# Two rings for attention weights in place of one, with the k/v ring 64 bytes lower in SBUF

## The chip, the cores and the metric

The kernel runs on one core of a Trainium2 chip. The metric is device microseconds of one execution, as the median of several runs; a profiled execution gives the trace that all lines below come from. The engines are TensorE (PE, with its weight loads shown as PEld), VectorE (DVE), ScalarE (ACT), GpSimd (POOL) and SyncE (SP), whose queue issues every DMA of this kernel. Each engine runs its own instructions in order and waits on semaphores for the others.

## What is computed

One transformer-like block on x of 2048 tokens by 1024 channels, in float32: a modulated layer norm, an attention with a compressive memory over four segments of 512 tokens (32 heads of 32), a gated residual, then a second modulated layer norm, a token-mixing MLP and a gated residual.

```python
mod = (_silu(c) @ w_mod)                       # six rows: sa, ca, ga, sb, cb, gb
h = _layernorm(x) * (1 + ca) + sa
# attention: q, k, v = h @ wq, h @ wk, h @ wv, 32 heads, 4 segments of 512
for s in range(4):
    p = softmax(qs @ ks.T * scale + mask)
    a_mem = (phi(qs) @ M) / (phi(qs) @ z + 1e-6)
    o = g * a_mem + (1 - g) * (p @ vs)
    M, z = M + phi(ks).T @ vs, z + sum(phi(ks))
x = x + ga * (o @ wo)
h = _layernorm(x) * (1 + cb) + sb
x = x + gb * (W2 gelu(W1 LayerNorm(h)^T + b1) + b2)^T
```

## The kernel before

**Precision.** A matrix that must be exact is kept as two fp32r halves, high and low: `split` (L116 to L123) copies the high half with one engine (L120 when that is ScalarE) and subtracts it with another (L123). A product is then three matmuls: high by high, high by low, low by high.

**Attention.** The heads are taken in 8 groups of four. `its` (L306) lists 32 projects: in pass 0 each group has segments 0 and 1, in pass 1 each group has segments 2 and 3. So the two projects 2g and 2g+1 use one set of weights, and a group comes back in the second pass.

- The normalised input lies in `page` tiles `h` (a ring of 16, 4 KB a partition each), as 8 chunks of 128 channels.
- `project` (L322) has four pieces. Pieces 0 and 1 compute k and v for half of the segment each: `kv_chunk` (L178) runs 48 matmuls at L185, with a 128x128 block of `h` stationary and 256 columns of the k/v weights moving (`nps`). Piece 2 transposes k (`kps`, L356), then `q_chunk` (L189) runs 24 matmuls at L193, with the q weights stationary and 512 columns of `h` moving (`qps`); k and q are split into `sg`, and `stack` (L312) sends parts of `sg` to the tiles `sk` with three DMAs a head. Piece 3 stacks the last head and works on the memory M.
- A step of the loop at L563 handles one head: `scores` (matmuls L446 to L453, exp on ScalarE, a mask and a second half on POOL, L457 and L461), `maxima` (L424, L425) for three steps ahead, `values` (L475) for the step before, and a piece of a project eight steps ahead.

**Weights.** A group has six weight tiles of 4 KB a partition, four for k/v (`v`, two parts of two) and two for q. They come from one ring of eight buffers (pool `paw`, tag `w`, L156). `load_w` (L168) is called four steps before the group's first project. In pass 0 `load_part` (L149) loads 512 KB into a `raw` buffer (a ring of three, shared with the loads of `token_tile`, `mod_late` and `wo_ahead`) and splits it into two tiles, each with a ScalarE copy and a VectorE subtract; `keep_w` (L163) then writes the six tiles to DRAM (`wsp`). In pass 1 the tiles are read back from `wsp` by the DMAs at L160. A tile of the ring may be written again only after the last matmul that reads its predecessor in the buffer.

**Addresses.** A pool is a stretch of SBUF, the same in every partition, and pools are stacked. `pad`, `pad2` (L71, L72) and `offset` are tiles that nothing reads or writes; they only shift what follows. `acst` holds `pad2` and small constants (mask, bd, csb, saca, MZ, bdg), and `paw` follows it.

**Order.** The kernel text gives the order in which instructions are recorded. A scheduler that works with its own model of times then interleaves them on each engine; `issue_after` and priorities bound it. So a changed dependency can move instructions that the diff doesn't touch. DMAs take eight semaphores in turn, and each waits for the eighth before it to be complete.

Of the kernel before, what the change touches and what calls it, by code (L numbers as in the profile page):

```python
# [7 lines left out]
F32 = mybir.dt.float32  # L8
F32R = mybir.dt.float32r
# [9 lines left out]
P = 128  # L19
# [25 lines left out]
def attention_and_mlp(ctx, tc, x, wq, wkv, wo, beta, w1, b1, w2, b2, c, wm_a, wm_b, out):  # L45
# [22 lines left out]
    acst = acst_pool.__enter__()  # L68
    top_pool = tc.tile_pool(name="top", bufs=1, side="right")
    top = top_pool.__enter__()  # L70
    top.tile([P, 8], F32, name="pad")  # L71
    acst.tile([P, 24], F32, name="pad2")  # L72
    psum = ctx.enter_context(tc.tile_pool(name="psum", bufs=1, space=PSUM))

    def bank(tag, bufs, name):
# [40 lines left out]
    def split(dst, src, hi_eng, lo_eng):  # L116

        hi, lo = dst[:, 0], dst[:, 1]
        if hi_eng is A:
            A.copy(hi, src)  # L120
        else:
            hi_eng.tensor_copy(hi, src)
        lo_eng.tensor_tensor(lo, src, hi.bitcast(F32), op=ALU.subtract)  # L123
# [20 lines left out]

    paw = tc.tile_pool(name="paw", bufs=1)
    aw = paw.__enter__()
    raw_w = {}

    def load_part(g, pr, kind, part, res):  # L149


        if pr == 0:
            r = a.tile([P, D], F32, tag="raw", bufs=3, name=f"raw{kind}{g}_{part}")
            SY.dma_start(r, (wkv if kind == "v" else wq)[g, :, 1024 * part:1024 * part + 1024])
        for i in range(2):
            w = aw.tile([P, 2, 512], F32R, tag="w", bufs=8, name=f"w{kind}{pr}_{g}_{part}_{i}")  # L156
            if pr == 0:
                split(w, r[:, 512 * i:512 * i + 512], A, V)
            else:
                SY.dma_start(w.bitcast(F32), wsp[g, 2 * part + i if kind == "v" else 4 + i])  # L160
            res[kind, 2 * part + i] = w
# [6 lines left out]
    def load_w(g, pr):  # L168
        res = W[pr, g] = {}
        for kind, part in (("v", 0), ("v", 1), ("q", 0)):  # L170
            load_part(g, pr, kind, part, res)
        if pr == 0:
            keep_w(g)
# [93 lines left out]
    for ct in range(NK):  # L267
        for part in range(2):
            wm = s1p.tile([P, D], F32, tag="wm", bufs=11, name=f"wm{ct}_{part}")
            last_wm = SY.dma_start(wm, wm_a[part, ct])  # L270
            if part == 0:
                V.scalar_tensor_tensor(wm, wm, 1.0, scb, op0=ALU.mult, op1=ALU.mult, accum_out=saca[:, ct, 0:1])
            else:
                for k in range(NK):
                    T.matmul(scale_ps[:, ct:ct + 1], wm[:, P * k:P * k + P], sc[:, k:k + 1], start=(k == 0),
                             stop=(k == NK - 1), skip_group_check=True)
        if ct < 3:
            load_part(0, 0, *(("v", 0), ("q", 0), ("v", 1))[ct], W[0, 0])
        V.tensor_scalar_add(saca[:, ct, 1:2], scale_ps[:, ct:ct + 1], 1.0)
        h_chunk(s1p, xs[0], 0, ct)  # L280
        if ct:
            first_chunk(ct - 1)
    first_chunk(NK - 1)
    left.__exit__(None, None, None)
    prj = tc.tile_pool(name="prj", bufs=1, reuse_waits="tile")
    pj = prj.__enter__()
    late = tc.tile_pool(name="late", bufs=1, reuse_waits="tile")
    b = late.__enter__()
    skp = [tc.tile_pool(name=f"sk{i}", bufs=1, reuse_waits="tile") for i in range(2)]
# [273 lines left out]
    for n in range(-LEADS, 4 * NI + VL):  # L563
# [19 lines left out]
        if 4 * NI - 5 <= m < 4 * NI + 3:  # L583
            i = m - 4 * NI + 5
# [5 lines left out]
        if n >= ML0 and (n - ML0) % MLS == 0 and (n - ML0) // MLS < 32:  # L590
            mod_late((n - ML0) // MLS)
    right.__exit__(None, None, None)
    for q in skp + [late, prj, paw]:
        q.__exit__(None, None, None)


# [6 lines left out]
    w = cw_pool.__enter__()  # L603
# [344 lines left out]
```

## Time and profile before

| | us |
|---|---|
| median of 3 runs | 2335.71 (2332.09 to 2339.83) |
| the profiled execution | 2329.09 |
| its span, first to last instruction | 2327.4 |
| TensorE busy in it | 2244.8 (96%) |
| VectorE, ScalarE, POOL busy | 1693.3, 1107.6, 721.8 |

Its mean granted TensorE clock is 0.983. TensorE's largest groups, mean time of one matmul from start to end (they are pipelined, so less than that lies between two starts):

| line | what | count | busy us | mean ns |
|---|---|---|---|---|
| L745 | the MLP's matmuls, 512 columns, three groups | 4704 | 535.6 + 431.7 + 164.5 | 389 |
| L185 | k and v, 256 columns | 3072 | 447.6 | 287 |
| L193 | q, 512 columns | 768 | 200.1 | 408 |
| L653 | output projection, 512 columns | 768 | 184.0 | 398 |
| L475 | probabilities by values, 97 or 65 columns | 2560 | 156.9 | 205 |

In the page's chain of what ended last, TensorE has 82% of the span, DMAs 6%, VectorE 6%. Attention runs to about 1020 us, the output projection to about 1200 us, and the MLP to the end.

A few times of single projects, from the trace: the k/v matmuls of project 3 end at 126.2 us, its q matmuls run from 145.7 to 152.0, and the q matmuls of project 4, the first of the next group, start at 173.3. In pass 1, the k/v matmuls of project 27 end at 898.5, its q matmuls at 907.4, and project 28's q matmuls start at 929.4.

### The profile page before, as it was taken

What the parts mean: (1) busy time and instruction counts of PE and PEld (TensorE: products, weight loads), DVE (VectorE), ACT (ScalarE), POOL (GpSimd) and SP (SyncE); (2) the same over time, 40 slices, a digit from 0 to 9 for tenths busy, and PEclk for the clock granted to TensorE, in tenths of its full rate; (3) what the DMA queues carried; (4) which work ended last, traced back from release to release, by engine and by line L of the source; (5) the groups of instructions that cost most, each with busy time, mean ns of one, the idle gap of its engine ahead of it and who ended that gap; (6) DMA issues with size and microseconds to landing.
All of it is one profiled execution on the core that took longest, in us unless ns stands there. A gap on an engine that the chain in (4) does not pass through costs nothing.

```text
span 2327.4 us, 38419 instructions
## 1 busy us (share of the span) xinstructions
PE 2244.8 (96%) x13866; PEld 1931.2 (83%) x13866; DVE 1693.3 (73%) x3806; ACT 1107.6 (48%) x2010; POOL 721.8 (31%) x827
## 2 busy tenths in 40 slices
PE   8999999999899999998989999999999999999999
PEld 7888888888789999986877888888888788888887
DVE  5666666785776566657889666598889787868687
ACT  5476766655566666655324333353335242424232
POOL 3165555675676555555000000023332000000000
PEclk9999999999999999999999999999999999999999
DMA  6747565788774444374354765465557542423233
GB/s 245 247 122 217 179 185 150 231 295 271 219 218 121 122 119 120 105 238 139 128 195 166 285 227 211 147 251 212 213 213 270 186 136 78 140 69 128 67 116 147
DMA packets 172593, 414.67 MB, mean 178 GB/s; under 512 B 17236, under 2 KB 71540, under 8 KB 163444
## 3 DMA queue, kind: packets, MB, share of 16 engines
q1 hardware_dynamic: 172404, 412.22, 53.3%
q8 instruction: 110, 1.80, 0.3%
q14 instruction: 79, 0.65, 0.1%
HBM read 236.23 MB, written 125.06 MB: 155 GB/s over the span
## 4 chain that ended last, share of the span: by engine, by line
PE 82%; DMA 6%; DVE 6%; ACT 2%; POOL 2%; issue 2%; SPq 1%; DVEq 0%; POOLq 0%; ACTq 0%
PE mx L745 44%; PE nps L185 12%; PE qps L193 7%; PE po L653 6%; PE pv L475 3%; PE sx L424 1%; PE a L446 1%; PE sz L424 1%; DMA rawx<-in_x_dram 1%; DMA rawm<-in_wm_b_dram 1%; PE a L449 1%; DMA wor<-in_wo_dram 1%; PE rd L396 1%; PE a L453 1%; PE up L406 1%
## 5 line engine op out<-in xcount | busy, mean ns | idle before, releaser
L745 PE MATMUL mx<-bU,sp 128*128 128x512 f32 x2352 | 535.6, 389 | 2.6 <-DVE sp L123 1.3
L745 PEld LDWEIGHTS mx<-bU,sp 128*128 128x128 f32 x2352 | 440.9, 188 | 96.8 <-DVE sp L123 2.1
L185 PE MATMUL nps<-wv,h 128*128 128x256 f32 x3072 | 447.6, 287 | 1.3 <-POOL h L123 1.1
L745 PE MATMUL mx<-bA,sp 128*128 128x512 f32 x1764 | 431.7, 389 | 3.4 <-DVE sp L123 1.8
L120 ACT CAST sp<-wr 128x384 fp32r<-128x384 f32 (+2 forms) x408 | 217.3, 545 | 445.5 <-PE mx L745 377.5
L461 POOL TENSOR_TENSOR ph<-p,ph 128x640 f16<-128x640 f32 x256 | 374.5, 1484 | 148.8 <-ACT ph L459 143.4
L185 PEld LDWEIGHTS nps<-wv,h 128*128 128x128 f32 x3072 | 409.8, 192 | 6.3 <-POOL h L123 1.3
L745 PEld LDWEIGHTS mx<-bA,sp 128*128 128x128 f32 x1764 | 330.7, 188 | 73.6 <-DVE sp L123 2.6
L123 DVE TENSOR_TENSOR sp<-wr,sp 128x384 fp32r<-128x384 f32 (+2 forms) x408 | 261.0, 651 | 33.7 <-ACT sp L120 33.2
L752 DVE TENSOR_TENSOR ac<-mx,ac 128x512 f32<-128x512 f32 x280 | 190.4, 689 | 91.0 <-PE mx L745 90.3
L193 PE MATMUL qps<-h,wq 128*128 128x512 f32 x768 | 200.1, 408 | 1.4 <-DVE r L349 1.3
L459 ACT CAST ph<-p 128x1280 f16<-128x1280 f32 x128 | 160.8, 1257 | 69.9 <-POOL p L457 69.3
L653 PE MATMUL po<-wo,ots 128*128 128x512 f32 x768 | 184.0, 398 | 8.1 <-DVE x L656 5.9
L653 PEld LDWEIGHTS po<-wo,ots 128*128 128x128 f32 x768 | 146.5, 192 | 40.1 <-issue 6.7
L193 PEld LDWEIGHTS qps<-h,wq 128*128 128x128 f32 x768 | 147.0, 197 | 31.8 <-issue 1.7
L457 POOL TENSOR_SCALAR_AFFINE_SELECT p<-p 128x256 f32<-128x256 f32 x256 | 126.1, 501 | 138.5 <-ACT p L454 88.4
L475 PE MATMUL pv<-vp,ph 128*128 128x97 bf16 (+1 forms) x2560 | 156.9, 205 | 10.8 <-POOL ph L461 4.5
L425 DVE CUSTOM_DVE_ANT_0 sx<-sx,mask 128x128 f32<-128x128 f32 (+1 forms) x256 | 110.5, 432 | 75.0 <-PE sx L424 73.8
L745 PE MATMUL mx<-bB,sp 128*128 128x512 f32 x588 | 164.5, 389 | 0.0
L475 PEld LDWEIGHTS <-ph 128*128 128x128 f16 x2560 | 121.0, 100 | 40.4 <-issue 17.1
L752 DVE TENSOR_TENSOR cc<-mx,cc 128x512 f32<-128x512 f32 x140 | 94.6, 685 | 53.4 <-PE mx L745 48.4
L745 PEld LDWEIGHTS mx<-bB,sp 128*128 128x128 f32 x588 | 110.3, 188 | 23.3 <-ACT bB L120 0.4
(173 smaller groups left out, 3184.6 us busy)
## 6 DMA issues: line engine op xcount, KB each, us to landing
sk<-sg SPq DMA_DIRECT2D x384, 128.0 KB
wr<-in_w_dram SPq DMA_DIRECT2D x28, 1024.0 KB
wr<-in_w_dram SPq DMA_DIRECT2D x32, 768.0 KB
bstu<-ucd SPq DMA_DIRECT2D x28, 768.0 KB
wsp<-wv SPq DMA_DIRECT2D x32, 512.0 KB
rawm<-in_wm_b_dram SPq DMA_DIRECT2D x32, 512.0 KB
wv<-wsp SPq DMA_DIRECT2D x32, 512.0 KB
pcd<-cc SPq DMA_DIRECT2D x14, 1024.0 KB
```

What stands on the lines that cost most here:

```text
L120: A.copy(hi, src)
L123: lo_eng.tensor_tensor(lo, src, hi.bitcast(F32), op=ALU.subtract)
L185: T.matmul(ps[:, aa], h[:, j, 128 * tt:128 * tt + 128], wt[:, i, o:o + 256], start=(n == 0), stop=(n >= 6 * NK - 2), skip_group_check=True)
L193: T.matmul(ps, wt[:, i, o:o + 128], h[:, j], start=(k + n == 0), stop=(3 * k + n == 3 * NK - 1))
L425: V.tensor_tensor_reduce(o, o, mask[:, 384 - 128 * i:], 1.0, -3.0e38, op0=ALU.add, op1=ALU.max, accum_out=mx[:, h % 2, i:i + 1])
L457: G.affine_select(w, w, pattern=[[0, 2], [1, 128]], compare_op=ALU.is_ge, fill=0.0, base=0, channel_multiplier=-1)
L459: A.copy(ph[:, 0], p32)
L461: G.tensor_tensor(ph[:, 1, c], p32[:, c], ph[:, 0, c], op=ALU.subtract)
L475: T.matmul(pv[:, i, 0:w], ph[:, part, o:o + 128], d["vp"][:, j, h, 0:w], start=(n == 0), stop=(n == 19), skip_group_check=True)
L653: T.matmul(ps, os_[:, i, P * ct:P * ct + P], wop[ct, nh][:, j], start=(n == 0), stop=(n == 3 * NK - 1))
L745: T.matmul(ps, ops[q][:, i, P * k:P * k + P], b[:, j], start=(m == 0 and first), stop=(m == 3 * nk - 1), skip_group_check=True)
L752: V.tensor_tensor(d, ps, d, op=ALU.add)
```

## The change

The one ring of eight becomes two pools: `paw`, now with six buffers for the k/v tiles, and after it `paq`, with an unused tile of 64 bytes and two buffers for the q tiles. `pad2` shrinks from 96 to 32 bytes, so what lies between it and the rings, and the k/v ring, starts 64 bytes lower; the unused tile puts the q ring and all behind it at the addresses they had.

```diff
-    acst.tile([P, 24], F32, name="pad2")
+    acst.tile([P, 8], F32, name="pad2")
...
     paw = tc.tile_pool(name="paw", bufs=1)
     aw = paw.__enter__()
+    paq = tc.tile_pool(name="paq", bufs=1)
+    awq = paq.__enter__()
+    awq.tile([P, 16], F32, name="pad3")
...
         for i in range(2):
-            w = aw.tile([P, 2, 512], F32R, tag="w", bufs=8, name=f"w{kind}{pr}_{g}_{part}_{i}")
+            w = (aw if kind == "v" else awq).tile([P, 2, 512], F32R, tag="w", bufs=6 if kind == "v" else 2,
+                                                  name=f"w{kind}{pr}_{g}_{part}_{i}")
...
-    for q in skp + [late, prj, paw]:
+    for q in skp + [late, prj, paq, paw]:
         q.__exit__(None, None, None)
```

## The prediction

> **What bounds the kernel now.** I read the table of stages first: busy time of each engine in four stretches, granted clock, DMA share, GB/s.
>
> ```profile
> core 0: us, PE busy (x) PEld busy (x) DVE busy (x) ACT busy (x) POOL busy (x), PEclk, DMA share, GB/s
> 100.00:700.00 600.00, 560.18 (x4687) 506.24 (x4686) 411.20 (x1213) 388.48 (x715) 367.70 (x405) 0.95 0.68 209
> 700.00:1010.00 310.00, 310.00 (x2759) 285.83 (x2757) 188.18 (x641) 192.65 (x339) 181.29 (x247) 1.00 0.45 127
> 1200.00:2327.00 1127.00, 1114.13 (x4899) 918.05 (x4897) 886.91 (x1461) 398.57 (x730) 96.88 (x60) 1.00 0.48 173
> ```
>
> TensorE (PE) ends last everywhere. From 700 to 1010 us (pass 1 of attention) it is never idle and its clock is 1.00: there only the speed of a matmul counts. From 100 to 700 (pass 0 and the start of pass 1) it is idle for 600 - 560.2 = 39.8 us and the clock averages 0.95: there a late producer shows. After 1200 us come the MLP's L745 matmuls, which touch no k, v or q weight.
>
> Next, the timeline of TensorE in pass 1, for the rate of one matmul. Columns: start, length, instruction, count.
>
> ```profile
> 814.76 4.04 PE L193 MATMUL qps<-h,wq 128*128 128x512 f32 x17
> 818.64 0.22 PE L452 MATMUL a<-sk 98*128 98x128 f32 x1
> ...
> 821.36 1.47 PE L185 MATMUL nps<-wv,h 128*128 128x256 f32 x11
> 822.67 0.34 PE L449 MATMUL a<-sk 98*128 98x384 f32 x1
> ```
>
> From the first start to the start of what follows: 17 q matmuls take 3.88 us, 228 ns each; 11 kv matmuls take 1.31 us, 119 ns each. 256 columns more cost 109 ns, so about 10 ns of each is not columns.
>
> Last, who makes and uses the q weights (name, median of one in ns between least and most, first and last start), and SyncE's (SP's) issues near one group change of pass 1.
>
> ```profile
> L193 PE MATMUL qps<-h,wq x768: 387/389/776, 28.0 to 1021.7; 128*128 128x512 f32 x192
> L120 ACT CAST wq<-rawq x16: 602/618/632, 18.7 to 462.9; 128x512 fp32r<-128x512 f32 x16
> L123 DVE TENSOR_TENSOR wq<-rawq,wq x16: 679/717/1506, 19.4 to 467.1; 128x512 fp32r<-128x512 f32 x16
> L160 SPq DMA_DIRECT2D wq<-wsp x16: 320/382/418, 536.5 to 956.9; - x16
> ```
>
> ```profile
> 898.76 0.86 SPq L160 DMA_DIRECT2D wq<-wsp  x2
> 899.99 0.32 SPq L493 DMA_DIRECT2D oT<-ot  x1
> 904.00 0.32 SPq L160 DMA_DIRECT2D wv<-wsp  x1
> 906.30 1.88 SPq L437 DMA_DIRECT2D sk<-nt  x3
> ```
>
> The two q loads went out at 898.76 and 899.2, as soon as the last k/v matmuls of project 27 had read the slots. The v load at 904.00 waited for a q tile of that project to be read: the one ring shows itself.
>
> **The change part by part.** *Work.* Each engine has the same instructions, none added or removed but waits; the two pads are allocated and never written. Cost 0.
>
> *Addresses.* All weights, the h pages and later tiles lie 224 bytes past a multiple of 256 now. The k/v ring moves to 160, the q ring stays at 224, and so does all behind. The small constants between pad2 and the rings (mask, bd, MZ, bdg) move by 64 bytes too. So the 3072 kv matmuls (L185) read moving weights and stationary h 64 bytes apart modulo 256; q matmuls as before. No fp32r matmul in this trace has its operands off the same residue, so this is bounded from both sides. The gain ends where the 10 ns above the columns are gone: 3072 x 10 = 31 us. For the loss I let that overhead double: 31 us. The nearest row is pv (L475), whose moving operand starts at many offsets against its stationary one: matching the trace's records to the program's addresses, the step from one 97-column matmul to the next has its median at 43 to 46 ns, differs with the address modulo 16 and not with the distance modulo 256. 64 is a multiple of 16. I take 0.
>
> The Trainium skill (TensorE: Matmul & The Clock Gate, "Step-by-step: what each phase is for") says that weight loads and moving data have two independent read ports, so that a load takes no bandwidth from a running matmul. By it this term is 0 for any distance. No run here shows fp32r operands 64 bytes apart.
>
> *The rings.* One ring of 8 held 6 tiles of a group and 2 to spare, the spare being the next group's first two v tiles. Now v has 4 and 2 to spare, q has 2 and none. So the next q tiles wait for the last q matmuls of the group's second project, not for its k/v matmuls; and the next-but-one group's first v tiles no longer wait for those q matmuls.
>
> In pass 1 the two loads of the row above wait for 904.0 and 907.4 (the last readers in project 27) instead: 5.2 and 8.2 us later. The next q matmuls start at 929.4. 1 MB at that stage's 127 GB/s is 8.3 us: there by 916, 13 us early. The new program places the first v loads ahead of them. Behind the waiting loads are two sk<-nt rows that come at 906.3 anyway; the second pair would be held 0 to 1 us, and their reader is several head steps on. Cost 0; without the 13 us it would be the lateness itself.
>
> In pass 0 a q tile is a ScalarE copy (0.62 us) and a VectorE subtract (0.72) from a raw buffer. There are six changes where the wait binds (groups 2 to 7). At before's times, the copies would be 1 to 26 us late, and stand in the new order inside the q matmuls of the group's second project, the second copy just ahead of the sg copy that reads those matmuls. The next q matmuls come some 21 us later (152.0 to 173.3 us between projects 3 and 4), so the tile itself is in time. What is queued behind pays: the ScalarE waits, held against before's end times of its neighbours, are 1.0, 1.1, 0.5, 3.4, 0 and 3.1 us; but the 3.4 is a place where ScalarE sat idle for 4.05 us on the same matmuls anyway. The other five average 1.1. So at most 6 x (0.62 + 0.72 + 1.1) = 15 us, if each us reached TensorE; at least 0, if the sg chain's slack hides it (the scores that need it come several head steps later). TensorE was idle only 40 of 600 us here, so most lands beside its work: I take a quarter, +4. If that cover is gone, the exp of the next scores (L447 to L454) is late, then POOL's L461, then pv.
>
> *The order.* The scheduler interleaves differently from about 129 us: some 6,800 of 16,170 TensorE program entries stand elsewhere, most by a few places, and almost none after 1200 us. It can give or take from the 40 us of idle time and the 30 us that a clock of 0.95 costs in that stretch (600 x 0.05). Bounds: a seventh of 70 either way, 10 us, as most entries keep their neighbours. I take 0.
>
> *Sum.* 0 + 0 + 0 + 4 + 0 = +4 us on the profiled execution's 2329.1 (span 2327.4): 2333. That execution is 6.6 us under the median of the runs, 2335.7; against that the time is 2340.
>
> **The rivals.** *B, the q split becomes the wait in pass 0.* All 15 us reach TensorE: 2335.7 + 15 = 2351. For it: ScalarE and VectorE are in-order, busy 388 and 411 of 600 us; a raw buffer held longer delays the rawm loads, for which VectorE waited 30.3 us in this stretch. Against it: the new order was made with that wait in it. It decides once a held-up copy outlasts the scores already queued for TensorE. The Trainium skill (same page, "What's actually happening") adds that an idle window of about 3.4 us halves the clock; the trace agrees so far that the clock is 1.00 where TensorE is never idle, 0.95 where it is idle 7%.
>
> *C, 64 bytes speed the kv matmuls.* Price up to 31 us; with two thirds of the 10 ns gone, -20: 2316. For it: fp32r matmuls of both lengths carry the same overhead, all with operands on one residue, and pv carries less (43 ns for 97 columns, which are 41 at the same rate). Against it: pv's indifference to distance.
>
> *D, the same 64 bytes slow them.* Half of 31, with the +4: 2356; the same facts, the other sign.
>
> *E, the new order or the earlier v tiles fill idle time.* -10: 2326. For it: v loads free of the q matmuls, and DMA waits in the chain (5.4 us on rawv at 194, 7.1 on rawm at 228). Against: raw buffers, not weight slots, held those.
>
> **How the numbers follow.** Forecast A 0.40 (2340), B 0.24, C 0.17, D 0.07, E 0.12. 0.3% is 7 us, about what a measurement of this kernel tells from no change (its runs span 2332 to 2340). Faster (under 2329): C, most of E, a little of A: 0.30. Slower (over 2343): B, D, a quarter of A: 0.41. Within: 0.29. The range of 8 in 10 leaves out the far ends of C and of B and D: 2313 to 2356. A alone would be 2333 to 2347.
>
> **What would show it.** The rate of kv matmuls in the timeline of pass 1: 119 to 121 ns confirms the address term, 108 to 116 is C, over 124 D. Idle time and clock from 100 to 700 us: about 44 us and 0.95 is A; 50 or more, with ScalarE or VectorE's wq lines waiting on L193's matmuls, is B; 30 is E. The wq loads of pass 1 must go out at the end of the q matmuls and the stage still have no idle time. I am wrong if the stage after 1200 us changes, or if 700 to 1010 gets idle time.

## The result and the profile after

The changed kernel takes 2343.98 us (median of 12 runs, 2338.18 to 2346.72), the kernel before 2334.06 (12 runs, 2330.72 to 2340.4). The ratio is 1.0037, interval 1.0025 to 1.0048: slower by some 8.6 us. The profiled execution has a span of 2336.5 us against 2327.4, and the same mean clock of 0.983.

First the stages of the changed kernel, the same columns as before the change: busy us of the five engines with their instruction counts, granted clock, DMA share, GB/s.

```profile
100.00:700.00 600.00, 550.99 (x4594) 493.88 (x4594) 401.86 (x1190) 381.25 (x700) 357.22 (x396) 0.95 0.67 206
700.00:1010.00 310.00, 307.54 (x2757) 282.47 (x2756) 190.66 (x644) 194.27 (x342) 181.76 (x246) 1.00 0.46 127
1200.00:2327.00 1127.00, 1118.02 (x4913) 920.34 (x4912) 886.70 (x1464) 398.94 (x730) 97.26 (x60) 1.00 0.49 174
760.00:1000.00 240.00, 240.00 (x2148) 220.62 (x2147) 144.57 (x494) 147.22 (x262) 137.37 (x190) 1.00 0.42 117
```

From 100 to 700 us TensorE is idle for 600 - 550.99 = 49.0 us, where it was 39.8: the loss arises there. How far one execution can be trusted for this shows in two later runs that leave the attention as it was and change the MLP alone: they have 41.8 and 42.2 us. Of the 2.5 us of idle time from 700 to 1010, 2.1 lie before 730 and belong to the stage before, which now reaches some 10 us further; from 760 to 1000 TensorE has none. (The row from 1200 on is not the MLP alone: the output projection's matmuls run from 1022 to 1247 us in the kernel before, beside the last steps of attention, and the MLP follows. The projection touches no k, v or q weight either.)

Next, TensorE in pass 1 of the changed kernel, to be held against the timeline of the prediction.

```profile
900.19 1.43 PE L189 MATMUL nps<-wv,h 128*128 128x256 f32 x11
901.45 1.06 PE L410 MATMUL up<-v,pk 128*128 128x132 f32 x8
...
910.17 3.36 PE L197 MATMUL qps<-h,wq 128*128 128x512 f32 x14
913.37 0.36 PE L479 MATMUL pv<-vp,ph 128*128 128x65 bf16 x6
```

Eleven kv matmuls take 1.26 us, 114.5 ns each (1.31 us, 119 ns, before); a q matmul 3.20 / 14 = 228.6 ns, as before. Single rows can miss a record, so all rates below are means over a kernel's whole trace: the records of TensorE put in order beside the program's matmuls with their addresses, steps from one start to the next within one kind, steps over 15% above the median left out. By that the kv matmul went from 119.4 to 115.9 ns, the q matmul from 229.1 to 228.8, the MLP's from 226.7 to 226.8.

Who makes and uses the q weights in the changed kernel (name, shortest, median and longest in ns, first and last start; then what its engine, and what others, waited for, with times):

```profile
L120 ACT CAST wq<-rawq x16: 601/620/627, 18.8 to 483.4; 128x512 fp32r<-128x512 f32 x16
L123 DVE TENSOR_TENSOR wq<-rawq,wq x16: 675/692/1899, 19.4 to 485.9; 128x512 fp32r<-128x512 f32 x16
...
  ACT wq L120: 10.2, 7
  PE qps L197: 9.0, 6
...
  ACT sg L120: 14.9, 5
```

The wait of the new ring is there: six times ScalarE's copy of a q weight waited for q matmuls, 9.0 us in all, and VectorE's subtract waited 10.2 us for such copies (9.3 of them from 100 us on). In the trace before, the copies waited 0.4 us from 100 us on, and for a kv matmul. But part of the new wait only stands where an old one stood. ScalarE's copies of the q results (`sg`) wait for the same matmuls; from 100 to 720 us, before and after:

```profile
ACT sg L120 <- PE qps L193: 9.8, 11, 4.1
ACT sg L120 <- PE qps L197: 6.6, 3, 4.2
```

(us in all, times, longest). With the 9.0 us, ScalarE waited 15.6 us for q matmuls where it waited 9.8: 5.8 us more, not 9.

Last, SyncE's issues of the changed kernel at the group change that the prediction looked at (project 27 to 28):

```profile
900.96 3.27 SPq L164 DMA_DIRECT2D wv<-wsp  x2
905.18 2.64 SPq L441 DMA_DIRECT2D sk<-nt  x4
907.92 0.86 SPq L164 DMA_DIRECT2D wv<-wsp  x2
...
913.11 0.32 SPq L164 DMA_DIRECT2D wq<-wsp  x1
...
916.76 0.39 SPq L164 DMA_DIRECT2D wq<-wsp  x1
```

The v loads go ahead, and the two q loads go out when project 27's q matmuls (which end at 916.5) have read each tile. The next q matmuls start at 938.25, so the second load, issued at 916.76, has 21 us.

Where the time goes, project by project: the end of a project's q matmuls, after minus before, in us, from one profiled execution of each. The two runs with an unchanged attention lie between 4.3 us early and 2.5 us late by this up to project 17, and are 0.8 to 2.4 us late from project 19 on.

| end of q matmuls of project | 3 | 7 | 9 | 12 | 16 | 17 | 18 | 19 | 22 | 31 | end of span |
|---|---|---|---|---|---|---|---|---|---|---|---|
| after minus before | -5.6 | +2.7 | -1.2 | +5.5 | +1.5 | +10.0 | +3.8 | +10.4 | +10.2 | +8.1 | +9.1 |

Up to project 16 the kernel wavers and is 1.5 us late in the end. At project 17 (its q matmuls end at 609.6 us before) it is 8.5 us later; the single ends still waver, as 18 shows, but from 19 on the loss stays. Then from 22 to 31, where TensorE is never idle, 2.1 us come back, 0.23 us a project: the faster kv matmuls.

### The profile page after: what moved, and what is told of

It is laid out like the page before. It is cut to its first block, busy times and chain, and to the rows that moved or that the text cites. A ratio compares the mean times of both kernels' runs of the same rounds, so it can differ in the third digit from the quotient of the medians.

```text
span 2336.5 us, 38402 instructions
## 1 busy us (share of the span) xinstructions
PE 2241.6 (96%) x13866; PEld 1922.3 (82%) x13866; DVE 1691.3 (72%) x3806; ACT 1108.1 (47%) x2010; POOL 719.7 (31%) x827
## 4 chain that ended last, share of the span: by engine, by line
PE 70%; DMA 12%; DVE 8%; POOL 3%; ACT 3%; issue 2%; SPq 2%; DVEq 0%; POOLq 0%; ACTq 0%
PE mx L749 37%; PE nps L189 11%; PE qps L197 6%; PE po L657 5%; PE pv L479 3%; DMA xb<-x1d 2%; DMA x1e<-xb 2%; POOL ph L465 2%; DMA rawm<-in_wm_b_dram 1%; DMA wr<-in_w_dram 1%; PE sx L428 1%; DVE bU L123 1%; PE sz L428 1%; PE a L450 1%; DMA wor<-in_wo_dram 1%
## 5 line engine op out<-in xcount | busy, mean ns | idle before, releaser
L189 PE MATMUL nps<-wv,h 128*128 128x256 f32 x3072 | 438.4, 284 | 1.5 <-POOL h L123 1.1
L189 PEld LDWEIGHTS nps<-wv,h 128*128 128x128 f32 x3072 | 401.7, 190 | 6.2 <-POOL h L123 1.3
L197 PE MATMUL qps<-h,wq 128*128 128x512 f32 x768 | 199.0, 407 | 0.3 <-DVE r L353 0.3
L197 PEld LDWEIGHTS qps<-h,wq 128*128 128x128 f32 x768 | 146.7, 197 | 30.1 <-DVE r L353 0.5
```

The source lines that it names most:

```text
L189: T.matmul(ps[:, aa], h[:, j, 128 * tt:128 * tt + 128], wt[:, i, o:o + 256], start=(n == 0), stop=(n >= 6 * NK - 2), skip_group_check=True)
L197: T.matmul(ps, wt[:, i, o:o + 128], h[:, j], start=(k + n == 0), stop=(3 * k + n == 3 * NK - 1))
```

## The experiments

All ratios are to the kernel before, with 95% intervals. "Order" is the order in which the scheduler puts the instructions on the engines; it was read from the built programs.

### The two parts alone: rings without the address, address without the rings

The rings alone: the changed kernel with `pad2` at its old size and without the second pad. Its order is that of the changed kernel.

```diff
-    acst.tile([P, 8], F32, name="pad2")
+    acst.tile([P, 24], F32, name="pad2")
...
-    awq.tile([P, 16], F32, name="pad3")
```

> The two rings without the 64 bytes: every tile at its address of before, every engine's order and every wait as in the changed kernel. Theory 1 (the address shift speeds the kv matmuls by 3.5 ns each, 119.4 to 115.9 in the two traces, and the rings with their new order cost some 19 us): the kv matmuls are 119 to 120 ns apart again, and the time is the changed kernel's plus 3072 x 3.5 ns = 11 us, a ratio to before of about 1.008 (2355 us). Theory 2 (the 64 bytes change nothing in the end, all of the loss is rings and order): the changed kernel's ratio, 1.004. Theory 3 (the rings are harmless and the address costs): 1.000.

The address alone: the kernel before, its one ring of eight 64 bytes lower. Its order is that of the kernel before. The q weights go along, so q matmuls too have their operands 64 bytes apart.

```diff
-    acst.tile([P, 24], F32, name="pad2")
+    acst.tile([P, 8], F32, name="pad2")
...
+    paq = tc.tile_pool(name="paq", bufs=1)
+    paq.__enter__().tile([P, 16], F32, name="pad3")
```

> One ring of eight as before, all of it 64 bytes lower, and 64 unused bytes behind it: orders and waits of before. Theory 1: kv matmuls 116 ns apart, 11 us less; the q matmuls, whose stationary operand is now the lower one, either gain too (768 x 3.5 ns = 3 us) or lose: ratio 0.994 to 0.996 (2320 to 2325). Theory 2: 1.000. Theory 3: 1.004 or more.

Measured: the rings alone 2347.81 us, 1.0062 (1.0042 to 1.0082), kv matmul 119.4 ns. The address alone 2329.91 us, 0.9985 (0.9972 to 0.9998), kv matmul 115.8 ns, q matmul 230.0. So the rings cost and the address gains, and the changed kernel stands between them. For the rings, theory 1 holds (its 1.008 is inside the interval, at the upper end; 1.004 is just outside). For the address, the rate came as theory 1 had it, but the time did not: 0.994 to 0.996 was expected. A row of the address alone, 1.26 us for eleven kv matmuls as in the changed kernel:

```profile
819.48 1.42 PE L187 MATMUL nps<-wv,h 128*128 128x256 f32 x11
820.74 0.34 PE L451 MATMUL a<-sk 98*128 98x384 f32 x1
```

Where the rest went: 3.6 ns on 3072 matmuls would be 11 us, and the q matmuls give back 0.9 x 768 = 0.7 us. But from project 21 to 31 all of the 2.4 us gained lie in the 809 steps from one kv matmul to the next, 3.0 ns each when the long ones are counted; steps to or from another kind gain next to nothing. That is 0.24 us a project and not 96 x 3.6 ns = 0.34. The profiled execution is 1 us ahead at project 16, 3.5 us ahead at the last q matmul and 0.9 us at the end of the span. So pass 0 keeps little of the gain; that other work than TensorE's sets the time there fits its idle time, but no run tests it. The address alone has the lowest median of this study; its interval ends just short of no change, and overlaps those of two later versions.

### How far the distance goes

The MLP's matmuls with their moving weights 64 bytes lower (a pad in the pool of the weights):

```diff
     bA = [b_tile(b3, 3, q, "bA0") for q in range(NPR)]
+    b3.tile([P, 16], F32, name="pad3")
```

> The kernel before with 64 unused bytes above the MLP's tiles bA and bU, so that these 4116 of its 4704 matmuls read a moving operand 64 bytes below their stationary one modulo 256. Orders and waits of before. Theory 1 as a property of every fp32r matmul: 226.7 ns apart become 223, 4116 x 3.5 ns = 14 us less, ratio 0.994. If only matmuls of 256 columns gain (where the weight load has less time): 1.000. Theory 3: above 1.

Measured: 2360.22 us, 1.0111 (1.0086 to 1.0136). TensorE in the MLP, before:

```profile
1505.06 3.34 PE L745 MATMUL mx<-bA,sp 128*128 128x512 f32 x14
1508.24 0.84 PE L745 MATMUL mx<-bB,sp 128*128 128x512 f32 x3
```

and with the pad:

```profile
1504.13 2.50 PE L746 MATMUL mx<-bA,sp 128*128 128x512 f32 x10
1506.47 0.40 PE L746 MATMUL mx<-bB,sp 128*128 128x512 f32 x1
```

From the first start to the next row's, 3.18 / 14 = 227 ns against 2.34 / 10 = 234. Over the whole trace 226.7 became 233.2 for bA and 233.3 for bU, which moved, on 4116 matmuls: 27 us, as much as the run lost (0.0111 of 2333 is 26). bB, whose operands stayed on one residue but stand between the others, went to 230.6, which is 2 us more. So the same 64 bytes that speed the kv matmuls of 256 columns slow the MLP's of 512: the other way than theory 1, and more than the 1.000 that was to show if only 256 columns gain.

Then all distances, in steps of 32 bytes: for the MLP a pad of 32 bytes before each of its seven weight buffers, for the attention weights ring tiles of 4128 bytes in place of 4096.

```diff
-    bA = [b_tile(b3, 3, q, "bA0") for q in range(NPR)]
+    bA = []
+    for q in range(NPR):
+        b3.tile([P, 8], F32, name=f"step{q}")
+        bA.append(b_tile(b3, 3, q, "bA0"))
```

> The kernel before with 32 unused bytes below each of the seven bA/bU tiles, so that in one run the moving operand lies 64, 96, 128, 160, 192, 224 and 0 bytes ahead of the stationary one modulo 256. Read in the distance between two starts, tile by tile. Theory 1: about 223 ns at 64 and 192, 226.7 at 0, and the other distances show where the effect begins. Theory 2: 226.7 at all.

```diff
-            w = aw.tile([P, 2, 512], F32R, tag="w", bufs=8, name=f"w{kind}{pr}_{g}_{part}_{i}")
+            w = aw.tile([P, 1032], F32R, tag="w", bufs=8, name=f"w{kind}{pr}_{g}_{part}_{i}")
+            w = w[:, 0:1024].rearrange("p (a n) -> p a n", a=2)
```

> One ring of eight as before, with 32 unused bytes behind each buffer, so that the eight buffers stand at all eight distances in steps of 32 bytes from the h pages modulo 256; orders and waits of before. For the kv matmuls (256 columns, weights moving) theory 1 expects 119.4 ns at 0 and 115.9 at 192, and this run shows where else the lower value holds. For the q matmuls (512 columns, weights stationary) it expects what the MLP's tiles showed: 226.7 at 0, 230 to 234 elsewhere. A theory by which only the distance 192 is special expects 119.4 at all others.

Measured, one profiled execution each (2351.59 and 2335.95 us), mean ns of a matmul by the distance of the moving from the stationary operand, modulo 256 bytes:

| distance | 0 | 32 | 64 | 96 | 128 | 160 | 192 | 224 |
|---|---|---|---|---|---|---|---|---|
| kv, 256 columns | 119.3 | 117.3 | 117.6 | 119.3 | 118.9 | 118.2 | 116.4 | 118.3 |
| q, 512 columns | 229.4 | 233.1 | 231.0 | 233.7 | 232.5 | 233.2 | 233.7 | 232.8 |
| MLP (bA), 512 columns | 229.4 | - | 231.2 | 234.1 | 232.5 | 233.9 | 233.0 | 233.3 |

For 256 columns 192 (64 bytes lower) is the best and 0 among the worst; for 512 columns 0 is the best, and theory 1's 223 ns at 64 and 192 did not show. The change gives each kind its best. In the q row the stationary operand was moved and in the MLP row the moving one, and the two rows agree within 1 ns: so it is the distance that counts there, not the address of one operand. For kv only the moving operand was moved. No run changes the number of columns alone, so that it is the columns which turn the sign is not shown: kv and the 512-column kinds differ in more than that. In these two kernels neighbours of other distances stand between, so the ends are softer than in the kernels with one distance each (115.8 and 226.7 ns).

### Where the rings cost: q's missing spare, pass 0, pass 1

Rings of five and three in place of six and two, so that q has a tile to spare (an edit to the kernel with the rings alone):

```diff
-            w = (aw if kind == "v" else awq).tile([P, 2, 512], F32R, tag="w", bufs=6 if kind == "v" else 2,
+            w = (aw if kind == "v" else awq).tile([P, 2, 512], F32R, tag="w", bufs=5 if kind == "v" else 3,
```

> Two rings at the addresses of before, five buffers for v and three for q in place of six and two: each kind has one tile to spare. If the loss of the rings (1.0062) is q's lack of a spare, at least half comes back: 1.003 or less. If it is what any reshuffle of this order costs, there is no such relation: near 1.006, or another value of either sign.

Two rings in one pass only: eight buffers named outright and dealt out in turn, from one list of eight or from two of six and two; addresses of before. `RINGS` says how many rings in pass 0 and in pass 1.

```diff
+RINGS = (1, 2)
...
-            w = aw.tile([P, 2, 512], F32R, tag="w", bufs=8, name=f"w{kind}{pr}_{g}_{part}_{i}")
+            s = slot_of[kind, pr, g, 2 * part + i]
+            w = aw.tile([P, 2, 512], F32R, tag=f"w{s}", bufs=1, name=f"w{kind}{pr}_{g}_{part}_{i}")
```

> Addresses of before; one ring in pass 0, two rings in pass 1 (each tile's buffer is named outright, by the same first-released rule). My prediction had pass 1 at nothing: 1.000 to 1.002. Rival: the loss arises where pass 1 begins and the DMAs are at 80%, as the 10 us between projects 16 and 17 in the trace suggest: about 1.004.

The other one has `RINGS = (2, 1)`.

> Addresses of before; two rings in pass 0, one ring in pass 1. My prediction had the whole cost here, so most of what e1 lost: about 1.005 to 1.006. Rival (the loss is at the beginning of pass 1): about 1.002.

Measured: five and three 2354.46 us, 1.0071 (1.0047 to 1.0095); pass 1 only 2334.08, 0.9991 (0.9977 to 1.0005); pass 0 only 2345.36, 1.0043 (1.0030 to 1.0056). The cost is that of pass 0, and pass 1 costs nothing that these runs can tell. A spare tile for q does not take it away. That is no clean test of the spare, though: v then has only one, and the trace still has 5.7 us of waits of q copies for q matmuls, with 5.3 us of waits for the raw q weights besides.

In every one of the runs with two rings in pass 0 much is lost at the border of the passes. From project 16 to 17 it is +8.5 us in the changed kernel, +10.0 with the rings alone, +5.5 with pass 0 only, +17.3 with five and three; from 16 to 22, where the ends have settled, +8.7, +10.9, +6.5 and +9.5. The two runs with the attention of before have +1.7 and +2.6 to there. What comes before project 16 differs: the rings alone are 7 us late by then, the changed kernel 1.5. No copy of a q weight stands there any more (in the changed kernel the last subtract starts at 485.9 us). What stands there, on VectorE of the changed kernel (last bracket: idle time before, and what ended it):

```profile
587.12 0.33 DVE L486 SCALAR_TENSOR_TENSOR am<-red,gate,pv 128x128 f32<-128x128 f32 x1
591.29 1.23 DVE L505 SCALAR_TENSOR_TENSOR rawm<-rawm,scb 128x1024 f32<-128x1024 f32 x1 [3.85 <-DMA rawm<-in_wm_b_dram]
...
592.44 0.56 DVE L429 CUSTOM_DVE_ANT_0 sx<-sx,mask 128x384 f32<-128x384 f32 x1
592.92 0.14 DVE L429 DVE_READ_ACCUMULATOR2_ANT mx<- 128x1 f32 x1
```

and on TensorE:

```profile
593.12 0.33 PE L428 MATMUL sx<-sk 96*128 96x128 f32 x1 [2.54 <-DVE mx L429]
```

VectorE waits 3.85 us for a load of `mod_late` into a raw buffer; the maxima of the scores stand behind it, and TensorE waits 2.54 us for those. The kernel before has such waits too: 30.3 us of VectorE on these loads from 100 to 720 us, 34.4 after, and at the border, from 560 to 720 us, 13.0 before and 12.2 after. So the loads do not keep VectorE longer there; but TensorE's waits for the maxima went from 3.6 to 7.0 us in that stretch, so what counts is what stands behind such a wait. This led to a second theory: not the rings' own waits cost, but the order that the scheduler makes of them.

### Waits or order: the same rings in other orders

A constant of the kernel (`ML0`, the head step of the loop at which the first of the 32 pieces of `mod_late` is put) reshuffles the attention without touching rings, addresses or work: with 13 each piece comes one step later, and 7439 of TensorE's 16170 instructions stand elsewhere.

```diff
-ML0 = 12
+ML0 = 13
```

One ring, this order:

> The kernel before with one constant of the planner changed (13 in place of 12: the loads of the late half of mod may start one head step later); one ring of weights, the same addresses, nothing computed otherwise. 7439 of the 16170 instructions of TensorE stand at another place in the order than before. It prices a mere reshuffle. Theory 'the rings cost by their own waits' (the copy of a q weight waits for q matmuls, 9 us of such waits in the changed kernel): no such wait is added here, the ratio to before is 0.999 to 1.001, and qps31 ends within 3 us of before's. Theory 'the rings cost by the order that the planner makes of them': a reshuffle of this extent moves the time as the rings did, the ratio is off by 0.002 or more to either side, and the difference arises before 700 us.

Two rings (at the addresses of before) with the same constant:

> Two rings at the addresses of before, with the planner's constant 13 in place of 12. Theory 'own waits': the pair with the one-ring kernel of that constant shows the same 1.005 to 1.007 again, and the waits of ScalarE's and VectorE's wq copies are again 6 to 10 us each. Theory 'order': the ratio of the pair is unrelated to 1.006 (0.997 to 1.010), and those waits may stand with no loss beside them.

Two rings with 11:

> Two rings at the addresses of before, with the planner's constant 11: a third order. Theory 'own waits': 1.005 to 1.007 of before, as with 12. Theory 'order': somewhere between 0.998 and 1.012, and where it is low, the jump of 10 us and more between the ends of the q matmuls of projects 16 and 17 is gone.

Measured:

| kernel | ratio | ScalarE's q copies wait for q matmuls, 100 to 720 us | project 16 to 17 |
|---|---|---|---|
| one ring, 12 (before) | 1 | 0 | 0 |
| two rings, 12 | 1.0062 (1.0042 to 1.0082) | 8.2 us | +10.0 |
| one ring, 13 | 1.0114 (1.0096 to 1.0131) | 0 | +21.8 |
| two rings, 13 | 1.0057 (1.0040 to 1.0074) | 13.3 us | +8.0 |
| two rings, 11 | 1.0021 (1.0008 to 1.0034) | 9.7 us | +6.7 |

The waits of the three two-ring rows (12, 13, 11), in the traces' words:

```profile
ACT wq L120 <- PE qps L196: 8.2, 7, 2.8
ACT wq L120 <- PE qps L196: 13.3, 7, 3.4
ACT wq L120 <- PE qps L196: 9.7, 8, 3.3
```

The constant alone, with one ring, costs more than the rings do. With the constant at 13 the two rings are faster than the one ring by 1.0057 / 1.0114 = 0.994 (0.991 to 0.998 from the ends of the two intervals), with 13.3 us of the new waits in the trace. So the theory that these waits cost 0.6% wherever they stand falls; with 11 the two rings are only 0.2% above the kernel before, but one ring with 11 was not run, so that row has no pair. Nor do ScalarE's waits for q matmuls order the times when those of its `sg` copies are added (9.8 us before; then 14.9, 19.6, 21.0 and 15.5 down the table). That another order makes such differences is shown, with one reservation: the constant also brings the pieces of `mod_late` later, and TensorE waits once for their result, 4.2 us with one ring and 2.1 us with two, which the kernel before does not. How much of the 0.4 to 0.6% of pass 0 is order and how much is waits is not shown, since every added dependency gives a new order, and a kernel with the waits in the order of before was not tried.

How one ring with 13 loses, in its windows at the border of the passes (columns as above):

```profile
560.00:700.00 140.00, 119.52 (x917) 106.73 (x916) 85.79 (x246) 68.94 (x119) 84.32 (x92) 0.88 0.71 220
```

and the kernel before there:

```profile
560.00:700.00 140.00, 128.32 (x1103) 115.78 (x1102) 98.13 (x285) 82.51 (x145) 94.90 (x104) 0.96 0.72 217
```

9 us more idle time, and the clock down from 0.96 to 0.88, which over 140 us are another 11: 20 us, where the step from project 16 to 17 grew by 22. This is one execution of each. Four other executions in the order of before have 0.95 to 0.98 in this window, so 0.88 stands apart; and over whole runs the mean granted clock is 0.975 in the four of this kernel, 0.980 in the 23 of the kernel before.

In the same window the changed kernel has 15.0 us of idle time, the kernel before 11.7, but the two-ring kernels with 13 and 11 have only 12.5 and 11.8. From project 16 to 22 these two lose 5.4 and 5.1 us, half of the 10.9 of the rings alone, and one ring with 13 loses 22.0. So the loss at the border changes with the order far more than with the rings.

### Both gains together

One ring in pass 0, two in pass 1, and the changed kernel's addresses (the six slots 64 bytes lower, two at the old place), as an edit to the kernel with two rings in pass 1 only:

```diff
-    acst.tile([P, 24], F32, name="pad2")
+    acst.tile([P, 8], F32, name="pad2")
...
-            w = aw.tile([P, 2, 512], F32R, tag=f"w{s}", bufs=1, name=f"w{kind}{pr}_{g}_{part}_{i}")
+            w = (awq if s in (6, 7) else aw).tile([P, 2, 512], F32R, tag=f"w{s}", bufs=1, name=f"w{kind}{pr}_{g}_{part}_{i}")
```

> One ring in pass 0 and two rings in pass 1 (that alone had 0.9991 of before, interval 0.9977 to 1.0005) with the addresses of the changed kernel: the six slots of k and v 64 bytes lower, the two of q at the old distance. Theory 'address gain and ring cost add up': k and v matmuls 115 to 116 ns, q 229.0 (the q matmuls of pass 0 in the lower slots 230), ratio 0.997 to 0.9985, about 2328 us. Rival 'the gain is taken back by waits in pass 0, only the stage that TensorE fills keeps it': 0.9985 to 0.9995.

Measured: 2331.85 us, 0.9993 (0.9979 to 1.0007). The rates came about as expected (kv matmuls in the lower slots 116.0 ns, q matmuls 229.6 and 229.8), the time did not: no better than the same kernel without the new addresses (0.9991). It is in the rival's range, but that waits in pass 0 took the gain is not shown by it. In its profiled execution the last q matmul ends 3.3 us earlier than before's and the output projection begins 3.3 us earlier, but the projection ends only 2.0 us earlier, and the span 0.7 us. From 1020 to 1230 us its clock is 0.94 against before's 0.96; the address alone, ahead by 3.5 us at the last q matmul and by 0.9 at the end of the span, has 0.93 there. Whether a shorter attention is given back in that stage by its clock in general is left open; these are single executions, and the runs of one kernel differ by more than that.

## Why the prediction was right, and where its terms were not

**The total** was right: 2344 against 2340, inside the range, and slower, as the likeliest of the three signs had it. That it lies so close is in part luck: the change was forecast at +4 us and measured at +8.6, the kernel before came out 1.6 us lower than in the first three runs, and two terms were off in opposite directions.

**What bounds the kernel** held. The loss arose between 100 and 700 us, where TensorE has idle time, and in the rest of attention only the speed of a matmul counted: 0.23 us a project come back there.

**Addresses, "I take 0": the step that failed in its reason.** The prediction argued from pv, "differs with the address modulo 16 and not with the distance modulo 256", as the nearest row. pv is bf16; the fp32r matmuls do depend on the distance. The kv matmul lost 3.5 of the "10 ns above the columns", which is rival C's mechanism, at 11 of its 31 us if every matmul kept it. By its own test ("108 to 116 is C") C was at work. In time the address alone is worth 0.9985 (0.9972 to 0.9998), 3.5 us, inside the bounds of 31 but not 0. The Trainium skill's rule (TensorE: Matmul & The Clock Gate, "Step-by-step: what each phase is for"), by which a weight load takes no bandwidth from a running matmul, would have given 0 for any distance; the MLP's 226.7 to 233.2 ns with nothing changed but the distance disagrees with that result, whatever the mechanism, which no run here shows.

**The rings, pass 1 "Cost 0"**: right, and for the reason given. The q loads went out at the end of the q matmuls, 21 us before use; TensorE stayed without idle time; two rings in pass 1 alone had 0.9991 (0.9977 to 1.0005).

**The rings, pass 0 "I take a quarter, +4", and the order, "I take 0": mis-sized.** The place was right: pass 0 alone costs 1.0043 (1.0030 to 1.0056), and the predicted waits are in the trace. Their sum is 9.0 us on ScalarE, where the prediction's add up to 9.1, but place by place they are 0.78, 1.75, 3.21, 1.45, 0 and 1.81 us against 1.0, 1.1, 0.5, 3.4, 0 and 3.1: the sum's closeness is luck. The prediction counted one wait as standing in place of an old one; in the trace 3.2 of the 9.0 us are made up for by shorter waits of the `sg` copies. But both terms together came to +10 us for pass 0 alone, and +14.5 for both rings alone (0.0062 of 2334), not +4. The step that failed is the small price: "so most lands beside its work" for the waits, and nothing for the order. The idle time is 49.0 us, just under the 50 that was to mark rival B, with the q copies waiting on those matmuls (L193 before, L197 now) as B has it. Still B is not shown: by the ends of the projects most of the loss falls after the last q copy, at the border of the passes. Nor is B excluded: of the 9.2 us of added idle time 5.9 lie before 560 us. The term that was too narrow is the order's, "a seventh of 70 either way, 10 us, as most entries keep their neighbours": one constant that leaves rings, addresses and work alone moved the time by 1.14%, 27 us. Which of the two terms holds the 14.5 us stays open.

**What follows for the sum.** In place of 0 + 4 + 0 = +4: address -3.5, rings and order +14.5, together +11, where the two kernels differ by 8.6; the intervals cover the difference.

**The tests for being wrong.** The MLP kept its rate, 226.8 ns. By the letter the second sign came up, 2.5 us of idle time from 700 to 1010; it is the end of the late stage before, and where only pass 1 runs there is none.

## What to carry to other kernels

The distance between the two operands of an fp32r matmul is worth trying by itself, for each shape by itself: an unused 64 bytes is all it takes, and here the best distance for 256 columns is among the bad ones for 512. A change of buffers under a scheduler is two changes, the dependency and a new order; price the order with a second reshuffle that adds no dependency before a gain or loss of 1% is put down to the dependency. And take a stage with no idle time for reading a rate, a stage with idle time for reading a wait.

## What the runs showed of the hardware

- The step from one fp32r matmul (with its own weight load) to the next depends on the distance of moving and stationary operand modulo 256 bytes, with opposite signs in the two kinds measured: kv, 256 columns, 119.4 ns at 0 and 115.8 at 192; MLP, 512 columns, 226.7 ns at 0 and 233.2 at 192.
- A loss in a stage with idle time can be larger than the idle time: in one execution of the reordered kernel with one ring 9 us more of it came with a clock of 0.88 in place of 0.96 over 140 us, another 11 us.
